# Products with the values moved directly ahead of the next pair's first transposes, and a late pair's transposes issued in two groups

## Chip, cores and metric

The kernel runs on one core of a Trainium2 chip. The metric is device time in microseconds, the median of several executions. One further execution was recorded by the hardware profiler, and its trace is what the rows below come from.

## What is computed

Three layers follow one another. Attention with a block mask (blocks of 64 positions) over 4 batches, 8 heads, 576 positions and 64 dimensions gives 2304 tokens of 512 values. A first MoE layer takes the elementwise maximum of three products and projects it. A second MoE layer routes each token to two of eight experts.

```
scores = q @ k.T / 8, masked to block_i >= block_j;  attn = softmax(scores);  a = attn @ v
x   = maximum(a @ w1, a @ w2, a @ w3) @ w_out
top2 of (x @ w_gate + log1p(exp(x @ w_noise)) * noise);  out = sum over 2 of w * (relu(x @ e1[e]) @ e2[e])
```

## The kernel before, in words

The work on attention is cut into 32 jobs. A job is a batch and a pair of heads, and is either early (the first 256 positions) or late (the positions from 256 on). Jobs 0 to 7 run in a first stage whose order a planner writes out. Jobs 8 to 31 run in the loop at line 1091, and only this loop changes. Their order is the list MIDDLE: `e2 l0 e2 e2 e2 l0 l0 e3 l0 e3 l1 e3 l1 e3 l1 l1 l2 l2 l2 l2 l3 l3 l3 l3`, 8 early and 16 late jobs (the letter, then the batch). The text calls a job of the loop a pair, for its two heads.

A late pair has five query blocks, 4 to 8. For each, `s_block` (line 330) makes the scores with three products (lines 314 to 316), takes the maximum on VectorE (line 320) and the exponential on ScalarE (line 321). `scale` (line 393) divides by the sums on VectorE (lines 395, 396, 400). `t_block` (line 405) transposes the block with TensorE into a PSUM bank (line 403) and copies it to SBUF on ScalarE (line 417, and line 420 on VectorE for a tail). The transposed blocks are the moving operand of `pv` (line 487), the products with the values, which `values` (line 464) issues at line 468: two heads side by side, each on 64 columns of the array. Its result is split in two parts by ScalarE (line 499) and VectorE (line 500) and becomes the input of a MoE unit; late rows of unit 8 are stored through DRAM (line 502). An early pair does the same with `s_early`, `t_early` (transposes at line 427) and `e_values`.

One pass of the loop treats pair j and the scores of pair j + 1. The lists `turn_steps(j)` (line 1042) and `score_steps(j + 1)` (line 1033) are issued alternately, one entry of each, and after each step comes `gap(j)` (line 1048). A gap issues filler: steps of the first MoE layer, generated by `chain` (line 1016), units 2, 4, 1, 6, 3, 5, 7 in this order. A step of `hidden` (line 801) is 24 products of 256 columns (lines 812 to 814) into one PSUM bank, emptied by ScalarE (line 817) or by a maximum on VectorE (line 819); a step of `columns` (line 831) is 18 products of 264 columns (lines 837, 838, 841). Each gap adds 1.0 (pairs 8 to 15) or 1.2 (later pairs) to a budget in the code's own units, and a step takes 2.6 or 2.0 of it. A unit can start only when all pairs of its batch are through, which the set `ready` tells. When no unit is ready, a gap stays empty.

Transposes, products with the values and the products of the filler take PSUM banks from one pool of four, `psT` (line 196). Scores have banks of their own. Loads and stores stand on SP's queue: queries and keys by `scored` (line 1065), values by `load_values` and `load_rest` behind `pv`, and a zero write of the output per pair by `init_out` (line 926). Outside the first stage the builder itself may place an instruction ahead of earlier ones when those are not ready; the code's order is its priority.

Of the kernel before, what the change touches and what calls it, by code (L numbers as in the profile page):

```python
# [38 lines left out]
def _jobs():  # L39
    n, o = {}, []  # L40
    for x in ["e0"] * 4 + ["e1"] * 4 + MIDDLE.split():
        o.append((int(x[0] == "l"), int(x[1]), n.get(x, 0)))
        n[x] = n.get(x, 0) + 1
    return o


JOBS = _jobs()
# [82 lines left out]
def tile_attention_moe_moe(ctx, tc, qT, kT, v, w1, w2, w3, w_out, gates, noise, e1, e2, out):  # L130
# [111 lines left out]
    def bank(kind="m"):  # L242
        n, c = TAGS[kind]
        return (psS if n == "s" else psT).tile([128, 512], F32, name=n, bufs=c)
# [17 lines left out]
    def load_scores(j):  # L262
        q = diagonal(SET[0][0])
        for r in range(2):
            nc.sync.dma_start(q[64 * r:64 * r + 64, :, 64 * r:64 * r + 64],
                              qT[at(j) + r, :, 0:256].rearrange("d (n c) -> d n c", c=64))
        load_keys(j, nc.sync)

    def load_rest(j, eng=None):
        (eng or nc.sync).dma_start(early_set(j)[2], v[at(j):at(j) + 2, :, :2].rearrange("h p c d -> p h (c d)"))  # L270

    def load_job(j):
        i = at(j)
        q = att.tile([128, 320], F32, name="rq")
        k = att.tile([128, S], F32, name="rk")
        nc.sync.dma_start(q, qT[i:i + 2, :, 256:S].rearrange("h d n -> (h d) n"))
        nc.sync.dma_start(k, kT[i:i + 2].rearrange("h d n -> (h d) n"))
        RAW[j] = q, k

    def load_values(j):  # L280
        n = LJ.index(j) % 2
        VV[j] = att.tile([128, 768 if n else 640], F32, name=("rv", "V")[n])[:, :640].rearrange("p (r c) -> p r c", r=2)
        nc.sync.dma_start(VV[j], v[at(j):at(j) + 2].rearrange("h p c d -> p h (c d)"))
# [19 lines left out]
    def prep_job(j):  # L303
        for low in (False, True):
            split_keys(j, low)
        for r in range(2):
            for low in (False, True):
                split_queries(j, r, low)
        RAW.pop(j)
# [20 lines left out]
    def s_block(j, i, c):  # L330
        st = new_stats(j)
        if i == 8:
            ps = psA[0].tile([128, 2, 512], F32, name="a2")
            for r in range(2):
                scores(ps[:, r, 0:288], j, i, 288 * r, 288 * r + 288)
            exps(st, c, ps[:, :, 0:288], PL[8][:, :576].rearrange("p (a b) -> p a b", a=2))
            return
        SB[i] = bank("s")
        ps = SB[i][:, :64 * i + 64]
        scores(ps, j, i, 0, 64 * i + 64)  # L340
        exps(st, c, ps, PL[i][:, :64 * i + 64])
# [32 lines left out]
    def s_early(j, h):  # L374
        e_scores(j, h)
        e_max(j, h)
        e_exp(j, h)

    def e_sums(j):
        st, z = ST[j][:, 1, 0:4], EPS[j, 1][:, 456:460]  # L380
        nc.vector.tensor_scalar(z, st, 1.0e-9, None, op0=OP.add)
        nc.vector.reciprocal(st, z)

    def e_scale(j, on):
        for i, c in EC.items():
            P = early_set(j)[3][:, POFF[i]:POFF[i] + 64 * i + 64]
            x = ST[j][:, 1, c:c + 1]
            if on != "ACT":
                (nc.vector if on == "DVE" else nc.gpsimd).tensor_scalar(P, P, x, None, op0=OP.mult)
            else:  # L390
                nc.scalar.activation(P, P, AF.Copy, scale=x)

    def scale(j, c0, blocks):
        st, z = ST[j][:, 1, c0:c0 + len(blocks)], SB[blocks[0]][:, 500:500 + len(blocks)]
        nc.vector.tensor_scalar(z, st, 1.0e-9, None, op0=OP.add)
        nc.vector.reciprocal(st, z)
        for c, i in enumerate(blocks):
            s = ST[j][:, 1, c0 + c:c0 + c + 1]
            P = PL[i][:, :64 * i + 64]
            nc.vector.tensor_scalar(P, P, s, None, op0=OP.mult)  # L400

    def turn(dst, i, key):
        nc.tensor.transpose(dst, PL[i][:, 128 * key:128 * key + 128], ident)

    def t_block(j, i, tail=None):
        if j not in PT:
            PT[j] = att.tile([128, 2, 4, 320], F32, name=("Ph", "Pl")[LJ.index(j) % 2])
        nk = (i + 2) // 2
        if i == 8:
            nk = 4  # L410
        ps = bank("t")
        for key in range(nk):
            turn(ps[:, 128 * key:128 * key + 128], i, key)
        if tail is not None:
            turn(ps[:, 384:512], tail, 4)
        o = 64 * SLOT[i]
        nc.scalar.activation(PT[j][:, :, :nk, o:o + 64].rearrange("p h k c -> p k h c"),
                             ps[:, :128 * nk].rearrange("p (k h c) -> p k h c", k=nk, h=2), AF.Copy)
        if tail is not None:
            nc.vector.tensor_copy(PT[j][:, :, 3, 192:256], ps[:, 384:512].rearrange("p (h c) -> p h c", h=2))  # L420
# [17 lines left out]
    def t_early(j, key):  # L438
        e_turn(j, key)
        e_copy(j, key, "DVE")  # L440
# [485 lines left out]
    def init_out(j):  # L926
        nc.sync.dma_start(out[256 * j:256 * j + 256].rearrange("(p t) (c d) -> p (t c) d", p=128, d=128),
                          zero[:, None, :].to_broadcast([128, 8, 128]))
# [83 lines left out]
    NJ = len(JOBS)  # L1012
# [11 lines left out]
    def filler(budget):  # L1024
        cost[0] += budget
        while cost[0] > 0:
            c = next(fill, None)
            if c is None:
                cost[0] = 0.0
                return  # L1030
            cost[0] -= c

    def score_steps(j):
        if j >= NJ:
            return []
        if LATE[j]:
            return [lambda: s_block(j, 4, 0), lambda: (s_block(j, 8, 1), scale(j, 0, (4, 8))),
                    lambda: s_block(j, 6, 2), lambda: (s_block(j, 7, 3), scale(j, 2, (6, 7))),
                    lambda: (s_block(j, 5, 4), scale(j, 4, (5,)))]
        return [lambda: s_early(j, 0), lambda: (s_early(j, 1), e_sums(j), e_scale(j, "ACT"))]  # L1040

    def turn_steps(j):
        if LATE[j]:
            return [lambda: (t_block(j, 4, 8), t_block(j, 8)), lambda: None, lambda: (t_block(j, 6), t_block(j, 7)),
                    lambda: None, lambda: t_block(j, 5)]
        return [lambda: (t_early(j, 0), t_early(j, 1))]

    def gap(j):
        filler(PER[j >= 16])
# [3 lines left out]
    def late_after(j):  # L1053
        return next((x for x in LJ if x > j), NJ)
# [4 lines left out]
    def following(j):  # L1059
        if j < 8:  # L1060
            x = next((x for x in range(j + 1, 8) if SETS[x] == SETS[j]), None)
            return x if x is not None else EJ[0] if SETS[j] == 0 else None
        return next((x for x in EJ if x > j), None)

    def scored(j):
        if LATE[j]:
            n = late_after(j)
            if n < NJ:
                prep_job(n)
                n = late_after(n)  # L1070
                if n < NJ:
                    load_job(n)
        elif following(j):
            load_scores(following(j))
# [13 lines left out]
    load_values(late_after(first))  # L1088
    scored(8)
    filler(4.0)  # L1090
    for j in range(8, NJ):
        b, g = JOBS[j][1:]
        T, SS = turn_steps(j), score_steps(j + 1)
        for n in range(max(len(T), len(SS))):
            if n < len(T):
                T[n]()
            if n < len(SS):
                SS[n]()
            gap(j)
        if j + 1 < NJ:  # L1100
            scored(j + 1)
        pv(j)
        if LATE[j]:
            n = late_after(j)
            if n < NJ:
                n = late_after(n)
                if n < NJ:
                    load_values(n)
        elif following(j):
            load_rest(following(j))  # L1110
        gap(j)
        gap(j)
        if j == 10:
            for tt in range(2):
                store(0, tt, C0[tt])
            late.append(route(0, C0["g"]))
        if all(x[:2] != JOBS[j][:2] for x in JOBS[j + 1:]):
            ready.add(2 * b + LATE[j])
        if 8 <= j < 8 + NU:
            init_out(j - 8)  # L1120
    ready.update(range(8))
    while 5 not in done:
        next(fill)
# [355 lines left out]
```

## Time and profile before

| | us |
|---|---|
| median of 3 executions | 974.41 (973.1 to 974.93) |
| the profiled execution, its own time | 970.67 |
| its span, first to last instruction | 968.9 |
| TensorE busy in the span | 957.8 |
| VectorE, ScalarE, GpSimd busy | 434.6, 432.5, 414.2 |

The span is what the views of the trace cover; 1.77 us of the execution lie around it. In a timeline row the first number is the start in us from the span's start, the second the duration. A matmul's duration is modelled and longer than the interval to the next start, since matmuls are pipelined, so what a product costs is read from starts.

### The profile page before, as it was taken

How to read it: one execution, taken by the hardware profiler on the slowest of the kernel's cores; microseconds unless marked ns; L12 is line 12 of the kernel's file. 1: busy time of each engine (PE TensorE's matmuls, PEld its weight loads, DVE VectorE, ACT ScalarE, POOL GpSimd, SP SyncE). 2: the span in 40 equal slices, each digit the busy share in tenths (PEclk: the TensorE clock that was granted, in tenths of full speed). 3: DMA queues.
4: the chain of work that ended last, by engine and by line, in shares of the span. 5: the costliest groups of instructions: out<-in, count | busy, mean ns of one | idle time of the engine just before them, and what ended most of it. 6: DMA issues, size and time to landing. Idle time of an engine off the chain costs nothing. (4 is left out here: it accounts for less than half of the span.)

```text
span 968.9 us, 17049 instructions
## 1 busy us (share of the span) xinstructions
PE 957.8 (99%) x6474; PEld 848.5 (88%) x6474; DVE 434.6 (45%) x1251; ACT 432.5 (45%) x968; POOL 414.2 (43%) x316
## 2 busy tenths in 40 slices
PE   9999999999999999999999999999999999999997
PEld 5866988999989898999999889898898979898895
DVE  7864756656567656643158331314141312222221
ACT  7487545555555545542125145444353434433110
POOL 2596201221322221222251487748565766755302
PEclk9999999999999999999999999999999999999999
DMA  9913822121121311303014459866758594753201
GB/s 325 346 31 94 232 71 73 47 87 53 60 71 47 102 50 41 113 15 123 21 57 154 127 170 235 186 168 179 176 169 182 168 201 143 189 140 124 62 16 56
DMA packets 113734, 118.75 MB, mean 123 GB/s; under 512 B 51164, under 2 KB 85980, under 8 KB 113648
## 3 DMA queue, kind: packets, MB, share of 16 engines
q1 hardware_dynamic: 102304, 88.51, 32.8%
q0 software_dynamic: 10224, 28.32, 10.2%
q8 instruction: 52, 0.85, 0.4%
q10 hardware_dynamic: 1120, 0.79, 0.3%
q14 instruction: 34, 0.28, 0.1%
HBM read 85.35 MB, written 25.24 MB: 114 GB/s over the span
## 5 line engine op out<-in xcount | busy, mean ns | idle before, releaser
L188 POOL TENSOR_TENSOR w<-rw,w 128x1536 fp32r<-128x1536 f32 (+1 forms) x42 | 131.9, 3145 | 65.5 <-ACT w L187 61.3
L828 POOL TENSOR_TENSOR hl<-hm,hh 128x512 fp32r<-128x512 f32 x21 | 27.5, 1309 | 147.4 <-ACT hh L827 146.8
L187 ACT ACTIVATE w<-rw 128x1536 fp32r<-128x1536 f32 (+1 forms) x42 | 55.9, 1344 | 74.4 <-DMA rw<-in_e 53.9
L1173 ACT ACTIVATE xg<-x 128x1024 uint16<-128x1024 uint16 x30 | 40.8, 1373 | 104.4 <-DMA x<-xg 102.9
L1199 PE MATMUL b<-xl,w 128*128 128x256 f32 (+4 forms) x272 | 83.5, 307 | 0.5 <-DVE xl L1189 0.5
L1200 PE MATMUL b<-xh,w 128*128 128x256 f32 (+4 forms) x272 | 83.4, 306 | 0.0
L1198 PE MATMUL b<-xh,w 128*128 128x256 f32 (+4 forms) x272 | 83.3, 306 | 0.0
L812 PE MATMUL t<-xA,w 128*128 128x256 f32 x288 | 83.0, 288 | 0.0
L813 PE MATMUL t<-xA,w 128*128 128x256 f32 x288 | 81.5, 283 | 0.0
L814 PE MATMUL t<-xA,w 128*128 128x256 f32 x288 | 81.3, 282 | 0.0
L1198 PE MATMUL t<-xh,w 128*128 128x256 f32 (+3 forms) x240 | 71.5, 298 | 0.2 <-DVE ht L1203 0.2
L1200 PE MATMUL t<-xh,w 128*128 128x256 f32 (+3 forms) x240 | 71.4, 298 | 0.0
L1199 PE MATMUL t<-xl,w 128*128 128x256 f32 (+3 forms) x240 | 71.3, 297 | 0.0
L1254 POOL DMA_INDIRECT out_rows<-y,isc x37 | 37.4, 1010 | 69.7 <-DVE y L1251 65.1
L812 PE MATMUL t<-xB,w 128*128 128x256 f32 x216 | 61.6, 285 | 0.0
L814 PE MATMUL t<-xB,w 128*128 128x256 f32 x216 | 61.1, 283 | 0.0
L813 PE MATMUL t<-xB,w 128*128 128x256 f32 x216 | 61.0, 282 | 0.0
L819 DVE TENSOR_TENSOR hm<-t,hm 128x512 f32<-128x512 f32 x48 | 33.1, 689 | 60.3 <-PE t L814 53.5
L852 POOL COPY xp<-x 128x1024 uint16<-128x1024 uint16 x18 | 19.4, 1076 | 88.7 <-ACT x L844 48.5
L1246 PE MATMUL b<-w,ht 128*128 128x512 f32 (+3 forms) x144 | 57.0, 396 | 0.0
L1248 PE MATMUL b<-w,ht 128*128 128x512 f32 (+3 forms) x144 | 56.9, 395 | 0.0
L1247 PE MATMUL b<-w,ht 128*128 128x512 f32 (+3 forms) x144 | 56.8, 394 | 0.0
(409 smaller groups left out, 2818.4 us busy)
## 6 DMA issues: line engine op xcount, KB each, us to landing
rw<-in_e SPq DMA_DIRECT2D x32, 768.0 KB
w<-in_w SPq DMA_DIRECT2D x18, 512.0 KB
rw<-in_e SPq DMA_DIRECT2D x16, 512.0 KB
rk<-in_kT SPq DMA_DIRECT2D x16, 288.0 KB
out_rows<-zero SPq DMA_DIRECT2D x9, 512.0 KB
x2d<-x SPq DMA_DIRECT2D x18, 256.0 KB
x2p<-xp SPq DMA_DIRECT2D x18, 256.0 KB
w<-in_w_out SPq DMA_DIRECT2D x6, 512.0 KB
```

What stands on the lines that cost most here:

```text
L187: nc.scalar.activation(t[:, 0, :c], r[:, :c], AF.Copy)
L188: nc.gpsimd.tensor_sub(t[:, 1, :c], r[:, :c], plain(t[:, 0, :c]))
L812: nc.tensor.matmul(ps[:, j], wh, x[:, 0], start=kt == 0, stop=False)
L813: nc.tensor.matmul(ps[:, j], wh, x[:, 1], start=False, stop=False)
L814: nc.tensor.matmul(ps[:, j], wl, x[:, 0], start=False, stop=kt == 3)
L1173: nc.scalar.activation(x.rearrange("p k t -> p (k t)").bitcast(U16).rearrange("p (c h) -> p h c", h=2), tp.rearrange("p (h k) t -> p h (k ...
L1198: nc.tensor.matmul(p, wt1(e, 0, kt, f), th[:, kt, c0:c1], start=kt == 0, stop=False)
L1199: nc.tensor.matmul(p, wt1(e, 0, kt, f), tl[:, kt, c0:c1], start=False, stop=False)
L1200: nc.tensor.matmul(p, wt1(e, 1, kt, f), th[:, kt, c0:c1], start=False, stop=kt == 3)
L1246: nc.tensor.matmul(ps, a, wt2(e, 0, f), start=f == 0, stop=False)
L1247: nc.tensor.matmul(ps, a, wt2(e, 1, f), start=False, stop=False)
L1248: nc.tensor.matmul(ps, l, wt2(e, 0, f), start=False, stop=f == 7)
```

## The change

The products with the values of pair j, with all that followed them in the pass (loads of values, the stores and the routing of unit 0 at j == 10, the mark that a unit is ready), move out of pass j into a function `values_of`. It is called at the start of pass j + 1, ahead of the first transposes, and once behind the loop. The two gaps that stood behind `pv` now stand ahead of it. The third and the fifth entry of a late pair's `turn_steps` become one, so the list has three entries: the blocks 4 and 8, nothing, the blocks 6, 7 and 5. A pass has as many steps as the longer list, so a pass of a late pair ahead of an early one (five) and the last pass have three steps instead of five.

```diff
     def turn_steps(j):
         if LATE[j]:
-            return [lambda: (t_block(j, 4, 8), t_block(j, 8)), lambda: None, lambda: (t_block(j, 6), t_block(j, 7)),
-                    lambda: None, lambda: t_block(j, 5)]
+            return [lambda: (t_block(j, 4, 8), t_block(j, 8)), lambda: None,
+                    lambda: (t_block(j, 6), t_block(j, 7), t_block(j, 5))]
         return [lambda: (t_early(j, 0), t_early(j, 1))]
...
-    for j in range(8, NJ):
+
+    def values_of(j):
         b, g = JOBS[j][1:]
-        T, SS = turn_steps(j), score_steps(j + 1)
-        for n in range(max(len(T), len(SS))):
-            if n < len(T):
-                T[n]()
-            if n < len(SS):
-                SS[n]()
-            gap(j)
-        if j + 1 < NJ:
-            scored(j + 1)
         pv(j)
         if LATE[j]:
             n = late_after(j)
...
         elif following(j):
             load_rest(following(j))
-        gap(j)
-        gap(j)
         if j == 10:
             for tt in range(2):
                 store(0, tt, C0[tt])
             late.append(route(0, C0["g"]))
         if all(x[:2] != JOBS[j][:2] for x in JOBS[j + 1:]):
             ready.add(2 * b + LATE[j])
+
+    for j in range(8, NJ):
+        b, g = JOBS[j][1:]
+        T, SS = turn_steps(j), score_steps(j + 1)
+        if j > 8:
+            values_of(j - 1)
+        for n in range(max(len(T), len(SS))):
+            if n < len(T):
+                T[n]()
+            if n < len(SS):
+                SS[n]()
+            gap(j)
+        if j + 1 < NJ:
+            scored(j + 1)
+        gap(j)
+        gap(j)
         if 8 <= j < 8 + NU:
             init_out(j - 8)
+    values_of(NJ - 1)
     ready.update(range(8))
```

## Rows read from the trace of the kernel before

**Rows 1.** The page, busy us (share of the span) and instructions of each engine.

```profile
PE 957.8 (99%) x6474; PEld 848.5 (88%) x6474; DVE 434.6 (45%) x1251; ACT 432.5 (45%) x968; POOL 414.2 (43%) x316
```

**Rows 2.** Busy time by stretch: length, busy us of each engine, granted clock, DMA.

```profile
97.00:440.00 343.00, 340.82 (x2719) 312.78 (x2718) 213.78 (x676) 180.13 (x481) 76.59 (x64) 1.00 0.26 75
```

**Rows 3.** TensorE's waits, 95 to 440 us: total us, times, longest.

```profile
PE s L314 <- DVE st L396: 1.0, 2, 0.7
PE t L403 <- DVE hm L819: 0.4, 1, 0.4
...
PE t L468 <- ACT Pl L417: 0.2, 1, 0.2
```

**Rows 4.** Timeline, TensorE: an early pair's values between MoE products.

```profile
189.83 0.28 PE L814 MATMUL t<-xA,w 128*128 128x256 f32 x1
190.04 0.87 PE L468 MATMUL t<-pte,kve 128*64 128x256 f32 x8
190.84 0.38 PE L812 MATMUL t<-xA,w 128*128 128x256 f32 x1
191.06 0.28 PE L813 MATMUL t<-xA,w 128*128 128x256 f32 x1
191.18 0.28 PE L814 MATMUL t<-xA,w 128*128 128x256 f32 x1
```

**Rows 5.** TensorE by line, 97 to 440 us: count, busy us, mean ns.

```profile
L468 PE MATMUL t<-Ph,rv 128*64 128x320 f32 (+2 forms) x160 | 18.4, 374 | 0.1
...
L468 PE MATMUL t<-pte,kve 128*64 128x256 f32 (+1 forms) x64 | 7.2, 340 | 0.1
```

**Rows 6.** Timeline, TensorE: eight transposes between MoE products.

```profile
423.05 1.03 PE L403 MATMUL t<-ident,p 128*128 128x128 f32 x8
423.84 0.36 PE L812 MATMUL t<-qe,w 128*128 128x256 f32 x1
424.04 0.28 PE L813 MATMUL t<-qe,w 128*128 128x256 f32 x1
```

**Rows 7.** Timeline, TensorE: values with eight transposes directly behind them.

```profile
147.57 0.87 PE L468 MATMUL t<-pte,kve 128*64 128x256 f32 x8
148.37 1.09 PE L403 MATMUL t<-ident,p 128*128 128x128 f32 x8
149.22 0.36 PE L812 MATMUL t<-xA,w 128*128 128x256 f32 x1
149.42 0.28 PE L813 MATMUL t<-xA,w 128*128 128x256 f32 x1
```

**Rows 8.** Timeline, TensorE: transposes between the halves of an early pair's values.

```profile
268.34 1.09 PE L403 MATMUL t<-ident,p 128*128 128x128 f32 x8
269.37 0.44 PE L468 MATMUL t<-pte,kve 128*64 128x128 f32 x4
```

**Rows 9.** Timeline, TensorE: the scores of block 7 ahead of late values.

```profile
416.70 0.39 PE L315 MATMUL s<-Kh,Ql 128*128 128x512 f32 x1
416.93 0.40 PE L316 MATMUL s<-Kl,Qh 128*128 128x512 f32 x1
417.37 2.28 PE L468 MATMUL t<-Ph,rv 128*64 128x320 f32 x20
```

**Rows 10.** Timeline, TensorE: three transposes (block 5) between MoE products.

```profile
430.56 0.49 PE L403 MATMUL t<-ident,p 128*128 128x128 f32 x3
430.81 0.37 PE L812 MATMUL t<-qe,w 128*128 128x256 f32 x1
431.01 0.28 PE L813 MATMUL t<-qe,w 128*128 128x256 f32 x1
```

**Rows 11.** Timeline, VectorE and TensorE: transposes wait for a bank.

```profile
359.04 0.69 DVE L819 TENSOR_TENSOR hm<-t,hm 128x512 f32<-128x512 f32 x1 [2.02 <-PE t L403]
...
359.78 0.66 PE L403 MATMUL t<-ident,p 128*128 128x128 f32 x4 [0.42 <-DVE hm L819]
```

**Rows 12.** Timeline, SP's queue: zero writes of the output.

```profile
103.95 4.27 SPq L927 DMA_DIRECT2D out_rows<-zero  x3
```

## The prediction

> **What bounds the kernel now.** I read the busy shares first. TensorE is busy for 957.8 of a span of 968.9 us [rows 1], so no other engine sets the end: time is won or lost only where TensorE's own stream gets shorter or gets a hole. Next I read the stretch in which the changed loop runs, about 97 to 440 us. TensorE is busy there for 340.82 of 343.00 us at the full granted clock (1.00, the 2.4 GHz level), VectorE for 213.78, ScalarE for 180.13 [rows 2]. Third come TensorE's waits in that stretch. Three lines hold 1.6 us in four waits: scores behind the statistics of softmax, transposes behind a PSUM bank, and 0.2 us of the products with the values behind a copy [rows 3]. So little is lost in plain waiting. What is left is the price of changing from one kind of product to another, which a busy share hides, because the ends of matmuls are modelled. For that I read start-to-start intervals in the timeline. In a run of MoE products one starts every 0.12 us [rows 4].
>
> **The change, part by part.**
>
> *1. Values directly ahead of transposes.* First the counts: late values products have two lines of 160 records, at 20 to a pair 16 late pairs, and 64 records at 8 to a pair are 8 early ones [rows 5]. That makes 24 groups, of which 23 have a next pair to be put against. The price of one group among MoE products: it starts 0.21 us after the product before it, 0.09 more than the steady 0.12; behind it the first product lasts 0.22 us until the second starts, 0.10 more than steady. From the group's start to the second product's start it is 191.06 - 190.04 = 1.02 us [rows 4]. Eight transposes among products take 424.04 - 423.05 = 0.99 us by the same reading [rows 6]. Where the kernel before happens to have values and eight transposes adjacent, both together take 149.42 - 147.57 = 1.85 us [rows 7]. Apart they are 1.02 + 0.99 less 0.12 for the product that is counted twice, 1.89 us. So adjacency saves 0.04 us. The groups touch transposes already in rows 7, in rows 8 and in one more place, so 20 groups are new: 20 x 0.04 = 0.8 us. The late group of 20 records has no clean twin with eight transposes behind it; I take the same price, since what differs is only what follows the group.
>
> As bounds: at best both ends of every group become free, 23 x (0.09 + 0.10) = 4.4 us. At worst nothing is saved, because the values still differ in kind from their new neighbour. They use the array as 128\*64 where transposes and all other products use 128\*128 (rows 4 and 7 show both forms), so each group still changes the form twice wherever it stands. The Trainium skill, page TensorEngine Tiling (Array Packing), Tiling Modes, Key Properties, says that changing the tiling mode drains TensorE; by that rule alone part 1 would save nothing, and the sum below would be 0.8 us smaller. The trace partly agrees: the price is there on both sides, and beside transposes it is only 0.04 lower. I stay with the measured 0.04.
>
> *2. Two more gaps between a pair's last transposes and its values.* Before, block 5's transposes stand at the end of the pair with only a scores block between them and the values. After, all of a late pair's transposes are out at its third step, and at least three gaps of filler lie between their copies and the values. The only named wait of the values, 0.2 us on ScalarE's copy, goes [rows 3]. Unnamed ones go too: the last 512-column scores product runs 0.44 us until the values start [rows 9]. A 512-column step is 0.23 us (the products before it), with the 0.09 of entry 0.32, so 0.12 was waiting. Between 0.2 us (the named wait alone) and 16 x 0.12 = 1.9 us I take 0.7, nearer the low end, because the view of waits names only one such wait.
>
> *3. Two groups of transposes instead of three.* Three transposes among products take 431.01 - 430.56 = 0.45 us, less one product 0.33, that is 0.11 for each; eight take 0.99 - 0.12 = 0.87, also 0.11 for each [rows 6, 10]. A group has no price of its own, so merging 16 times saves 0. Bounds: 0 and, if its entry cost as much as that of values, 16 x 0.09 = 1.4 us.
>
> *4. Banks.* Products, transposes and values all take PSUM banks of one kind, of which there are four. Blocks 6, 7 and 5 now take three in a row, so the products behind them need the bank of the products just ahead of them, where before one more bank lay between. That bank is freed by VectorE's maximum (or ScalarE's copy). Once in the kernel before that maximum comes late and the second of two transposes groups waits 0.42 us for it [rows 11]. I count one more such wait, +0.4 us. The bounds are 0 (the bank is free in time, as nearly always now) and 16 x 0.42 = 6.7 us. Values plus two transposes banks also make three in a row, but the values alone run 2.28 us [rows 9], which covers the maximum's 0.69 [rows 11].
>
> *5. What else moves.* The evacuation of the values (two ScalarE copies, two VectorE subtractions for a late pair) and the copies of the next transposes now come in one burst. VectorE and ScalarE are 62% and 53% busy [rows 2], and the filler behind covers them; without that cover it is the bank price of part 4. On SP's queue the values' loads, the store of the late rows and, once, four stores of the first unit move two gaps back, past one zero write of the output per pair; those writes are already issued far ahead of their place (three of them at 103.95 us [rows 12]), so nothing new stands in front. The loaded values are needed one pair later by an early pair, two later by a late one, a distance that is the same as before. POOL's two plane copies for the first unit move with their stores, and nobody reads them until the expert stage. Cost 0. The loop has 162 gaps before and 150 after (a late pair ahead of an early one, and the last pair, lose two each). By the code's own prices 5.2 us less filler is emitted in the loop. It runs later in an unbroken stretch, at the same 0.12 us each: 0.
>
> Sum: -0.8 - 0.7 + 0 + 0.4 = **-1.1 us**. The profiled execution took 970.67 us (span 968.9 and 1.77 around it) and would take 969.6. The median of the runs, 974.41, stands 3.7 us above it; carried over, **973.3 us**. A measurement of this kernel can tell about 0.2%, 1.95 us, from no change, so the forecast is "no difference".
>
> **The rivals.**
>
> *Faster, 971.2 us.* The order is loosened enough that all 1.6 us of waits of rows 3 go, and the merged transposes do save half of part 3's bound, with nothing paid back: -0.8 (part 1) - 1.6 - 0.8 = -3.2. For it: the pairs 20 and 21, where by the code's prices the filler has run dry for seven gaps, get filler again, because units are used more slowly. Against it: the first line of rows 3 is scores that wait for softmax statistics; the change leaves those where they are and takes the three transposes away that stood ahead of late scores as cover.
>
> *Slower, 978.4 us.* The bank mechanism of part 4 decides. If the products behind blocks 6, 7 and 5 wait 0.34 us in each of 16 pairs, +5.4 less 1.5 gives about +4. It passes the 0.2% bound from (1.95 + 1.5) / 16 = 0.22 us per pair. For it: rows 11 show that the maximum can queue behind scaling and evacuation, which the change bunches. Against it: once in 16 pairs now.
>
> *The change does not do what it says, 974.4 us.* The emitted order is not what the engines get: in the trace a later pair's eight transposes stand between the two halves of an early pair's values [rows 8], though the text has them apart. If the builder goes on placing whatever is ready, values and transposes may be parted again. Against it: most groups stand where the code puts them, and all inputs of both groups are long ready.
>
> **How the numbers follow.** Forecast 0.40 (all within 0.2%), faster 0.31, slower 0.14, not as written 0.15 (0.12 within, 0.02 faster, 0.01 slower). That gives faster 0.33, same 0.52, slower 0.15. The range runs from the faster rival with some of part 1's upper bound, 970.6, to half of the slower rival with the spread of the shown runs, 976.4. It leaves out most of the slower rival and the far end of the other.
>
> **What would show it.** Right: values start 0.21 us behind a MoE product, the transposes follow without a product between, 20 or more such pairs; the stretch of the loop shorter by about 5 us of filler plus 1 us; the total of waits about as before. Part 3 right: 11 transposes at 0.11 us each. Part 4 wrong: waits of products on hm's maximum, over 0.2 us a pair. The prediction is wrong if adjacency saves over 0.1 us a group, or if a new wait over 2 us in sum shows in that stretch.

## The result, and the profile after

The change made the kernel slower. The median of 20 runs is 977.0 us (972.8 to 985.35), beside 970.61 us (968.73 to 979.84) in 20 runs of the kernel before on the same chip. The ratio is **1.0053, 95% interval 1.0034 to 1.0072**: 0.53%, or 5.1 us. The two medians by themselves lie 6.4 us apart; the text goes by the ratio and its interval. The first three of the 20 runs of the kernel before are those of the table ahead of the prediction (median 974.41), and they lie above 16 of the other 17. Forecast was -0.11%, with a range that ended at +0.2%. The profiled execution took 980.67 us, its span is 978.8 us. That is 10.0 us more than the profiled execution of the kernel before, about twice what the ratio gives, so sums read from these two profiles overstate the loss.

The page's busy times and the windows come first, as in [rows 1, 2].

```profile
PE 960.0 (98%) x6474; PEld 851.9 (87%) x6474; DVE 437.2 (45%) x1251; ACT 429.7 (44%) x968; POOL 413.5 (42%) x316
```

```profile
97.00:440.00 343.00, 338.37 (x2701) 312.46 (x2700) 215.08 (x674) 177.39 (x479) 75.71 (x64) 1.00 0.26 75
```

In the loop's 343 us TensorE is busy 2.45 us less than in [rows 2]. The span grew by 9.9 us and the busy time by 2.2, so most of what is new is holes. The view of TensorE's waits names them. First the loop, 95 to 500 us, as in [rows 3] (total us, times, longest), then the expert stage, 500 to 970 us.

```profile
PE s L315 <- DVE Ql L301: 2.8, 2, 1.5
PE t L403 <- DVE xA L485: 1.1, 1, 1.1
PE s L314 <- DVE st L396: 0.4, 1, 0.4
PE t L812 <- DVE hm L819: 0.3, 1, 0.3
...
PE t L1205 <- DVE ht L1210: 3.5, 2, 2.0
PE b L1205 <- DVE xB L1210: 1.4, 1, 1.4
PE b L1205 <- ACT xh L1195: 0.6, 1, 0.6
...
```

Two things are new in the loop. Scores (L315, the product with the low part of the queries) wait 2.8 us in two waits for the split of the queries on VectorE, line 301, and one group of transposes (L403) waits 1.1 us for VectorE's line 485. The wait of the values for a copy is gone, as forecast. No line of the prediction names the split. The same view of the kernel before has it, in a fourth row that [rows 3] and the prediction's "three lines" leave out:

```profile
PE s L315 <- DVE Ql L301: 0.2, 1, 0.2
```

The expert stage, whose code the change doesn't touch, has more waits too; they come last below.

Here is the first of the two waits, in the timeline: TensorE, then VectorE, then GpSimd. It also shows the adjacency that the change is for.

```profile
145.94 0.34 PE L315 MATMUL s<-Kh,Ql 128*128 128x384 f32 x1
146.12 0.34 PE L316 MATMUL s<-Kl,Qh 128*128 128x384 f32 x1
146.29 0.53 PE L841 MATMUL t<-w,hl 128*128 128x264 f32 x3
146.75 0.87 PE L468 MATMUL t<-pte,kve 128*64 128x256 f32 x8
147.55 1.09 PE L403 MATMUL t<-ident,p 128*128 128x128 f32 x8
148.40 0.39 PE L314 MATMUL s<-Kh,Qh 128*128 128x320 f32 x1
148.63 0.29 PE L314 MATMUL a<-Kh,Qh 128*128 128x288 f32 x1
150.18 0.41 PE L315 MATMUL s<-Kh,Ql 128*128 128x320 f32 x1 [1.26 <-DVE Ql L301]
...
147.44 2.69 DVE L301 SCALAR_TENSOR_TENSOR Ql<-rq,Qh 64x320 fp32r<-64x320 f32 x2 [0.39 <-ACT Qh L299]
...
147.13 1.41 POOL L292 TENSOR_TENSOR Kl<-rk,Kh 128x576 fp32r<-128x576 f32 x1 [4.38 <-ACT Kh L289]
148.48 1.30 POOL L852 COPY xp<-x 128x1024 uint16<-128x1024 uint16 x1
```

How to read it: the split queries of all late pairs share one pair of buffers, so the next late pair's queries can't be split until the last scores of the late pair before (145.94 and 146.12) have read them. Then follow ScalarE's copies and VectorE's two subtractions (`prep_job`, L289 to L301). The next scores need both. In between TensorE has three products, the values and eight transposes as cover, 2.7 us from the L315 at 145.94 to the L314 at 148.63. The two subtractions end at 150.13. An undisturbed one takes 0.49 us (median of the 30, below); these two took 2.69 together. The first lies beside GpSimd's subtraction of the keys, and the second ends 0.35 us behind GpSimd's plane copy (148.48 + 1.30 = 149.78). The other of the two waits, at 271 us, has the same form.

In the kernel before, the same place has the values and eight transposes of [rows 7], and behind them nine MoE products (149.22 to 150.36). Its split was held up as well, but the scores waited almost nothing:

```profile
150.36 0.31 PE L314 MATMUL s<-Kh,Qh 128*128 128x320 f32 x1
...
150.99 0.42 PE L315 MATMUL s<-Kh,Ql 128*128 128x320 f32 x1 [0.18 <-DVE Ql L301]
...
148.91 2.03 DVE L301 SCALAR_TENSOR_TENSOR Ql<-rq,Qh 64x320 fp32r<-64x320 f32 x2 [0.67 <-ACT Qh L299]
```

So the delay was there all along, 2.03 us for two splits, and the filler covered it, though barely: of the 15 late pairs whose queries are split in the loop of the kernel before, three have the split ready only 0.05, 0.05 and 0.25 us before the scores that need it (ends and starts in its trace). The Trainium skill, page SBUF — State Buffer, section Who interferes with whom, says that a VectorE instruction with two SBUF inputs contends with a GpSimd instruction that reads SBUF, and that one of the two blocks fully until the other has ended. The split has two SBUF inputs, and the rows agree, since it is held until GpSimd is through.

### The profile page after: what moved, and what is told of

Same layout as the page of the kernel before. It is cut to its first block, busy times and chain, and to the rows that moved or that the text cites. A ratio compares the mean times of both kernels' runs of the same rounds, so it can differ in the third digit from the quotient of the medians.

```text
span 978.8 us, 17044 instructions
## 1 busy us (share of the span) xinstructions
PE 960.0 (98%) x6474; PEld 851.9 (87%) x6474; DVE 437.2 (45%) x1251; ACT 429.7 (44%) x968; POOL 413.5 (42%) x316
## 5 line engine op out<-in xcount | busy, mean ns | idle before, releaser
L828 POOL TENSOR_TENSOR hl<-hm,hh 128x512 fp32r<-128x512 f32 x21 | 27.1, 1289 | 169.4 <-ACT hh L827 169.4
L1210 DVE SCALAR_TENSOR_TENSOR ht<-t,ht 128x256 fp32r<-128x256 f32 (+3 forms) x56 | 25.9, 462 | 70.9 <-ACT ht L1209 70.9
```

## The experiments

Every ratio below is to the kernel before on the same chip, with its 95% interval; five rounds each unless said.

### The parts of the change alone

**The values moved, the transposes as before.** The change, with the three groups of transposes put back.

```diff
-            return [lambda: (t_block(j, 4, 8), t_block(j, 8)), lambda: None,
-                    lambda: (t_block(j, 6), t_block(j, 7), t_block(j, 5))]
+            return [lambda: (t_block(j, 4, 8), t_block(j, 8)), lambda: None, lambda: (t_block(j, 6), t_block(j, 7)),
+                    lambda: None, lambda: t_block(j, 5)]
```

> Only the move of the values is made; a late pair's transposes stay in three groups. Lost cover (values and transposes now stand where filler stood between the split of the queries and the next scores, so TensorE waits for VectorE): ratio 1.003 to 1.007 to before, and waits of TensorE on the split queries (line 301) of 2 us or more in the loop. Banks or the merged transposes as the cause: 0.998 to 1.001, no such waits. Any new order costs in the expert stage: 1.002 to 1.006, with the loss behind 500 us.

Measured 967.65 us, ratio **0.9968 (0.9952 to 0.9983)**: faster than both kernels, and outside all three ranges that were expected. One wait for the split is there, and no wait in the expert stage.

```profile
PE a L315 <- DVE Ql L301: 1.2, 1, 1.2
```

**The merged transposes in the order of before.** The same edit of `turn_steps` as the change, in the kernel before.

> Only the merge of a late pair's transposes into two groups is made (with the two gaps fewer that follow from it for six pairs); the values stay where they were. Lost cover: 0.998 to 1.002, waits in the loop as before, under 2 us. Three banks in a row as the cause: 1.004 to 1.007, with waits of transposes or products on hm's maximum (line 819) of over 2 us. Any new order costs in the expert stage: 1.002 to 1.006, with the loss behind 500 us.

Measured 974.19 us, ratio 1.0034 (1.0019 to 1.0049); there is no wait on `hm`, by which banks would have shown. Here the price takes another form. With two gaps fewer in six pairs, and the values still at the end of the pass, the values come right behind the copies of the block just transposed:

```profile
PE t L468 <- ACT Pl L417: 1.3, 1, 1.3
PE t L468 <- ACT Ph L417: 1.1, 1, 1.1
```

**The change with the twelve gaps given back.** Two empty steps stand behind the merged group, so that a late pair has five steps again and the loop 162 gaps.

```diff
-                    lambda: (t_block(j, 6), t_block(j, 7), t_block(j, 5))]
+                    lambda: (t_block(j, 6), t_block(j, 7), t_block(j, 5)), lambda: None, lambda: None]
```

> The change with two empty steps added to a late pair's list, so that the loop has 162 gaps as before. Fewer gaps as the cause: back to 0.998 to 1.001. Lost cover: 1.002 to 1.006, since the gaps stand ahead of the values either way and the waits on line 301 stay. Any new order costs in the expert stage: 1.002 to 1.006 with the loss behind 500 us.

Measured 973.2 us, ratio 1.0023 (1.0004 to 1.0042). So the change's +5.1 us splits, at about 971 us, into -3.1 (values), +5.3 (merge: 1.0023 against 0.9968) and +2.9 (the missing gaps: 1.0053 against 1.0023). By the intervals each of the last two is uncertain by about 2.5 us. The scores wait for the split four times, and behind ScalarE's half of it once:

```profile
PE s L315 <- DVE Ql L301: 2.2, 4, 1.0
...
PE s L314 <- ACT Qh L299: 0.5, 1, 0.5
```

**Less filler ahead of the loop.** In the kernel before, `filler(4.0)` ahead of the loop became `filler(1.4)`, which shifts the phase of the filler's steps.

> The kernel before with 1.4 in place of 4.0 units of filler ahead of the loop, one MoE step less there; nothing else. Any new order costs in the expert stage: 1.002 to 1.006 here too, with the loss behind 500 us. Lost cover or banks: 0.998 to 1.002, neither is touched.

Measured 972.05 us, ratio 1.0008 (0.9992 to 1.0025): no difference. This one shift of phase does not bring the loss; others were not tried.

### GpSimd's part: one operation moved

**The plane copies on ScalarE**, in the change and in the kernel with the values alone moved. They are the operation that held up the second split above.

```diff
-        nc.gpsimd.tensor_copy(planes, x2.bitcast(U16).rearrange("p (d h) -> p h d", h=2))
+        if u == NU - 1:
+            nc.gpsimd.tensor_copy(planes, x2.bitcast(U16).rearrange("p (d h) -> p h d", h=2))
+        else:
+            nc.scalar.activation(planes, x2.bitcast(U16).rearrange("p (d h) -> p h d", h=2), AF.Copy)
```

> The change, with the plane copy of units 0 to 7 (line 852) on ScalarE in place of GpSimd. VectorE held up by GpSimd (split queries of 1.4 us twice in a row where Kl and the plane copy follow each other): no split query over 1.5 us and none that follows a second one of over 1 us because of line 852; waits of TensorE on line 301 fall from 2.8 us to under 1.5; ratio to before 1.001 to 1.004. Only the order counts: waits of the same size on line 301 or elsewhere in the loop, 1.004 to 1.007.

> Only the move of the values, and the plane copy of units 0 to 7 on ScalarE. VectorE held up by GpSimd: as fast as the move alone or 1 us faster, 0.995 to 0.998. Only the order counts, or ScalarE's 25 us more are felt: 0.998 to 1.002.

The change went from 1.0053 to 1.0027 (1.001 to 1.0043), at 972.33 us; the wait for the split fell from 2.8 to 1.3 us. The values alone gained nothing, 0.9984 (0.9967 to 1.0002). By the waits the copy is part of the price, not all of it; the ratios point the same way, but the intervals of the change with and without the edit overlap.

**Both kernels once more**, unchanged, one profile each, to see which waits repeat.

> The changed kernel once more, for a second profile. The loss behind 509 us comes from the built order: again 6 us or more between the first transposes of expert 0 and the last expert, with waits on line 1210 at the same products. It varies with each execution's transfers: 2 to 5 us, at other products; the loop's waits on line 301 (2.8 us) are as before in both cases.

> The kernel before once more, for a second profile. Loss from the built order: waits in the expert stage under 1 us again. It varies with each execution's transfers: up to 3 us of them. Waits in the loop 1.8 us as before in both cases.

The change again took 2.8 us in two waits on L301, 1.1 on L485. The kernel before again had no such wait over 0.2 us, but now 3.1 us in one wait of L1198 on `ht` in the expert stage. The loop's waits repeat; the expert stage's come and go in both kernels.

### Merge or gaps

**Block 5 one step earlier, but in a step of its own.** The values moved, 162 gaps; the edit is shown against the kernel with the values alone moved. From the change with its gaps given back it differs in one thing: block 5 comes one step later, so that the scores of block 6 and a gap part it from the blocks 6 and 7.

```diff
-                    lambda: None, lambda: t_block(j, 5)]
+                    lambda: t_block(j, 5), lambda: None]
```

> The values moved as in the change; three groups of transposes as before, but block 5's comes one step earlier, straight in the step behind that of the blocks 6 and 7 (162 gaps). It stands between the run that moves the values alone (ratio 0.9968) and the change with two empty steps appended (1.0023), and differs from the second only in that one gap of filler parts block 5 from 6 and 7. If the merge costs because eleven transposes and three banks come in one step: ratio near 0.997, 0.995 to 0.999. If it costs because block 5's transposes no longer stand as cover ahead of the next pair's last scores, whatever they are grouped with: near 1.002, 1.000 to 1.004, with the scores' wait for VectorE's split of the queries (L301) at 2 us or more in the loop.

Measured 967.13 us, ratio **0.9972 (0.9956 to 0.9988)**. So it costs nothing that block 5 leaves its place ahead of a pair's last scores. What costs is what parts this kernel from the change with its gaps given back: block 5 put together with 6 and 7. Whether that is the merge itself, or that block 5 then comes two steps early, was not told apart: an unmerged block 5 two steps early with 162 gaps was not run. The scores' wait on L301 is gone. The timeline of both kernels at one pair shows why. First the change with its gaps given back, then this one, from the last scores of one late pair to the first of the next (in this one the products between 269.81 and 273.40 are left out).

```profile
270.34 0.34 PE L316 MATMUL s<-Kl,Qh 128*128 128x384 f32 x1
270.64 1.03 PE L403 MATMUL t<-ident,p 128*128 128x128 f32 x8
272.18 0.42 PE L314 MATMUL s<-Kh,Qh 128*128 128x320 f32 x1 [0.50 <-ACT Qh L299]
...
273.68 0.42 PE L315 MATMUL s<-Kh,Ql 128*128 128x320 f32 x1 [0.96 <-DVE Ql L301]
```

```profile
269.52 0.34 PE L316 MATMUL s<-Kl,Qh 128*128 128x384 f32 x1
269.81 1.03 PE L403 MATMUL t<-ident,p 128*128 128x128 f32 x8
...
273.40 0.31 PE L314 MATMUL s<-Kh,Qh 128*128 128x320 f32 x1
...
273.80 0.31 PE L315 MATMUL s<-Kh,Ql 128*128 128x320 f32 x1
```

From the last scores to the next it is 1.84 us with the merge, 0.50 of it a wait, and 3.88 without. Here 23 filler products stand behind the eight transposes (270.60 to 273.40); with the merge the filler comes only at 276.9 us, behind the first scores of the next pair. Filler comes in steps of 24 or 18 products, and the two kernels differ in the side of those first scores on which one step falls. By what rule the builder places it there is not shown.

**Three groups in three consecutive steps.** Again shown against the kernel with the values alone moved: nothing merged, but a late pair has three steps and the loop 150 gaps, as in the change.

```diff
-            return [lambda: (t_block(j, 4, 8), t_block(j, 8)), lambda: None, lambda: (t_block(j, 6), t_block(j, 7)),
-                    lambda: None, lambda: t_block(j, 5)]
+            return [lambda: (t_block(j, 4, 8), t_block(j, 8)), lambda: (t_block(j, 6), t_block(j, 7)),
+                    lambda: t_block(j, 5)]
```

> The values moved; three groups of transposes, unmerged, but in three consecutive steps, so that a late pair has three steps and the loop 150 gaps, as in the change. If the twelve gaps that go cost by themselves (the change without them is 0.3% faster than with them): 1.000, between 0.998 and 1.002, and the first transposes of expert 0 come 0.8 to 2 us later against the last filler than with 162 gaps. If the gaps cost nothing and the merge all: 0.997, 0.995 to 0.9985, loop waits under 2 us.

Measured 973.72 us, ratio 1.0034 (1.0011 to 1.0056), outside what was expected on either side. The gaps cost by themselves, and 0.66% here, so the split above into merge and gaps depends on the order in which they are taken: with the gaps first it is 6.4 us for them and 1.8 for the merge. The loop's waits on these two lines are nearly those of the change:

```profile
PE s L315 <- DVE Ql L301: 2.8, 2, 1.5
PE t L403 <- DVE xA L485: 0.8, 1, 0.8
```

**Amount or place of the filler.** In the kernel just shown each gap's budget times 1.08; in the kernel with the values alone moved, times 150/162.

> The values moved, three groups of transposes in three consecutive steps (150 gaps, ratio 1.0034), each gap's budget 1.08 times larger, so that the loop emits as much filler as with 162 gaps. If it is the amount of filler in the loop that costs: near the 162-gap kernels, 0.995 to 0.9985. If it is the place of the gaps (a late pair ahead of an early one has two gaps fewer between its values and the next scores, or the transposes stand closer): 1.001 to 1.005, with the scores' wait on L301 still over 2 us in the loop.

> The values moved, transposes as before (162 gaps, ratio 0.9968), each gap's budget cut to 150/162, so that the loop emits as little filler as with 150 gaps. If the amount costs: 1.000 to 1.004. If the place of the gaps costs: 0.995 to 0.9985.

Measured 1.0001 (0.9985 to 1.0017), between the two ranges expected, and 0.998 (0.9959 to 1.0). Giving the amount back recovers about half; taking it away costs 0.12%, which the intervals don't tell from nothing. Neither reading is enough alone.

### GpSimd's work out of the loop

Four orders, each with the keys' subtraction (L292) and the low part (L828) given to VectorE and the plane copies (L852, units 0 to 7) to ScalarE as above, and the kernel before with the same edit as control.

```diff
-            nc.gpsimd.tensor_sub(QK[j][1], k, plain(QK[j][0]))
+            nc.vector.tensor_sub(QK[j][1], k, plain(QK[j][0]))
...
-            (nc.vector if u == NU - 1 else nc.gpsimd).tensor_sub(l, m, plain(a))
+            nc.vector.tensor_sub(l, m, plain(a))
```

> The values moved, transposes as before, and the loop's GpSimd work on SBUF (the keys' subtraction L292, the low part L828, the plane copies of the units 0 to 7) given to VectorE, VectorE and ScalarE. Nothing is left out. VectorE then has some 36 more operations of about 0.5 us each but none held up by GpSimd. If VectorE held by GpSimd is what makes scores wait: L301 takes about 0.5 us everywhere, no wait on it in the loop; ratio 0.995 to 0.998 beside 0.9968 with GpSimd. If VectorE becomes too full: waits on maxima and splits, ratio over 0.999.

> The same three pieces of GpSimd's work moved away in the change with two empty steps appended (162 gaps, merged transposes, ratio 1.0023). If the merge costs because it brings scores up to where VectorE is still held by GpSimd: within 0.2% of the run of the values alone without GpSimd's work, so 0.995 to 0.999, and the waits on L301 (2.2 us) are gone. If the merge costs through banks, order or the cover of scores whatever GpSimd does: 0.4% to 0.6% above that run, 1.000 to 1.003.

> The three consecutive steps with 150 gaps (1.0034) with the loop's GpSimd work on SBUF given to VectorE and ScalarE. With 162 gaps and without that work the ratio was 1.0000. If the missing gaps cost because scores come up while GpSimd holds VectorE: within 0.2% of that, 0.998 to 1.002, no wait on L301. If they cost in another way (order around the last units, the expert stage): 1.003 to 1.008.

> The whole change (1.0053) with the loop's GpSimd work on SBUF given to VectorE and ScalarE. If GpSimd holding VectorE is what both the merge and the missing gaps cost by: 0.998 to 1.002. If only the merge costs by it and the gaps by something else: 1.002 to 1.005. If neither: over 1.005.

> The kernel before with the loop's GpSimd work on SBUF given to VectorE and ScalarE, the control for the four variants with the same edit (0.9986 to 1.0007). If GpSimd's work costs only where scores are late by the change, the edit brings the kernel before nothing or a small loss: 1.000 to 1.004, and the change then counts as 0 to 0.4% faster on that ground. If the edit itself is worth the 0.5 to 0.7% that it brought the change, independent of the order: 0.993 to 0.996.

| order | GpSimd as it is | its work moved |
|---|---|---|
| before | 1 | 1.0008 (0.9988 to 1.0028) |
| values moved | 0.9968 | 1.0000 (0.9978 to 1.0021) |
| values, merge, 162 gaps | 1.0023 | 1.0007 (0.9987 to 1.0027) |
| values, no merge, 150 gaps | 1.0034 | 1.0002 (0.9984 to 1.002) |
| the change | 1.0053 | 0.9986 (0.997 to 1.0001) |

On the left the four changed orders lie 0.85% apart, on the right 0.21%, less than their intervals. The edit by itself brings the kernel before nothing. So the merge and the gaps cost only together with GpSimd's work. One wait on L301 is left among these five, 0.6 us in the order without the merge. That the values alone lose their 0.3% with this edit was not expected (0.995 to 0.998 was); with the merge and 162 gaps, too, the ratio lies above the 0.995 to 0.999 expected for this cause, though within 0.2% of the values alone, as was expected. VectorE has more to do then, and the loop has one new wait, 0.9 us of early scores (L356) behind L485; why the gain goes stays open.

**The keys' subtraction alone** given to VectorE, in the change; the other two stay on GpSimd.

> The change with the keys' subtraction alone (L292) given to VectorE; the low part L828 and the plane copies L852 stay on GpSimd. If the split of the queries is late because it runs beside that one subtraction: the wait on L301 (2.8 us in two, up to 1.5) goes and the ratio is 0.9985 to 1.002, as with all three moved. If the other two hold VectorE as much (L400 of 3.2 us behind L828): 1.002 to 1.005, with the wait of L403 on xA (1.1) still there.

Measured 969.98 us, ratio **0.9987 (0.9966 to 1.0007)**: one line takes back the whole loss. The kernel before with this one line moved was not run; with all three pieces moved it is 1.0008. It is the cleanest of the runs, because TensorE's order at the pair shown above stays the same (the three products L841 left out):

```profile
144.38 0.34 PE L315 MATMUL s<-Kh,Ql 128*128 128x384 f32 x1
...
145.19 0.87 PE L468 MATMUL t<-pte,kve 128*64 128x256 f32 x8
145.99 1.09 PE L403 MATMUL t<-ident,p 128*128 128x128 f32 x8
...
147.07 0.29 PE L314 MATMUL a<-Kh,Qh 128*128 128x288 f32 x1
147.20 0.41 PE L315 MATMUL s<-Kh,Ql 128*128 128x320 f32 x1
...
145.47 0.76 DVE L292 TENSOR_TENSOR Kl<-rk,Kh 128x576 fp32r<-128x576 f32 x1
146.15 1.00 DVE L301 SCALAR_TENSOR_TENSOR Ql<-rq,Qh 64x320 fp32r<-64x320 f32 x2
```

The cover is the same 2.7 us (144.38 to 147.07), but keys and queries together are through in 1.68 us (145.47 to 147.15), and nothing waits. All 30 splits of the stretch now take the same time, first the change, then this kernel (ns: least, median, most):

```profile
L301 DVE SCALAR_TENSOR_TENSOR Ql<-rq,Qh x30: 472/490/1592, 111.1 to 404.3; 64x320 fp32r<-64x320 f32 x30
```

```profile
L301 DVE SCALAR_TENSOR_TENSOR Ql<-rq,Qh x30: 475/484/492, 110.1 to 397.9; 64x320 fp32r<-64x320 f32 x30
```

### What stays open: the expert stage

The traces tell how much of the loss lies in the loop. Here the loop is counted from its first scores to the first transposes of expert 0, and the rest from there to the end of TensorE's last product (us, from starts in the traces; the two kernels each have two profiles).

| kernel | loop | behind it |
|---|---|---|
| before | 410.5 and 409.6 | 453.5 and 458.9 |
| the change | 412.6 and 411.8 | 462.1 and 457.9 |
| the change, keys' subtraction on VectorE | 407.4 | 455.3 |
| before, GpSimd's work moved | 410.7 | 456.0 |
| the change, GpSimd's work moved | 407.7 | 456.1 |

The loop's part of the loss is 1.3 to 3.0 us. The rest of the 5.1 lies outside it, and behind the loop two profiles of one kernel differ by 4 to 5 us. With GpSimd's work moved in both, the change's loop is 3.0 us shorter than the other's, which is the direction that was forecast; each is one profile, and the intervals of the ratios (0.9986 and 1.0008) overlap.

In the change 6.4 us of waits stand behind 500 us, 0.7 in the kernel before. One of them, 2.0 us, is ScalarE's queue: a copy of expert weights stands ahead of the `relu` that TensorE needs, and waits for the weights.

```profile
649.33 1.38 ACT L1180 ACTIVATE xg<-x 128x1024 uint16<-128x1024 uint16 x1 [8.22 <-DMA x<-xg]
650.57 2.41 ACT L187 ACTIVATE w<-rw 128x1024 fp32r<-128x1024 f32 x2
...
659.09 1.49 ACT L187 ACTIVATE w<-rw 128x1536 fp32r<-128x1536 f32 x1 [5.47 <-DMA rw<-in_e]
660.48 0.46 ACT L1209 ACTIVATE ht<-t 128x368 fp32r<-128x368 f32 x1
```

ScalarE had stood 8.22 us for gathered rows before that, and the weights' own read (line 174) could start only when the subtraction on GpSimd that follows these copies (line 188) had freed a buffer, at 654.12. A wait of this kind, 3.1 us, stands in the second profile of the kernel before too, so it is not the change's alone. It is longer than 0.6 us in neither of the two kernels at 0.997. With GpSimd's work as it is, the waits behind 500 us add up to 1.1 to 6.4 us in five profiles with 150 gaps and to 0 to 3.3 in seven with 162, so the ranges overlap. Whether the missing gaps make them likelier, and how, was not tried.

## Why the prediction was wrong

**Part 1 was right.** Values stand directly ahead of transposes 21 times (20 or more were forecast), they start 0.21 us behind a product, and the values moved alone make the kernel 0.32% faster. That is 3.1 us where the sum had 1.5 for parts 1 and 2. Whether the sizes were right is not shown: in its profile the loop (from the first scores at 96.84 to the first transposes of expert 0 at 506.38) takes 409.5 us, 1.0 less than in the first profile of the kernel before (98.31 to 508.81) and no less than in the second.

**Part 2 was right as to its wait:** no wait of L468 is left.

**Part 3 is the step that failed, and part 5 with it.** Part 3 costed the merge at 0, with bounds of 0 and 1.4 us of gain, from the price of a transposes group on TensorE (0.11 us each). That price is right. The merge costs 5.3 us nonetheless, as measured with 162 gaps. No loss was put into the bounds, because the step asked only what the instructions cost and not what a new order does to the work that covers a wait. What the runs show in its place: less work of TensorE between one late pair's last scores and the next scores (at the pair above 1.84 us, where it is 3.88 with block 5 in a step of its own), less than the split of the queries needs beside GpSimd (3.3 us there, from the last scores to its end). The prediction had come near: its faster rival says that the change "takes the three transposes away that stood ahead of late scores as cover". It gave that no price, and it is not quite the cover that counted: with block 5 taken from the last scores, but in a step of its own, the kernel stays at 0.9972.

**Part 4 had the right kind of wait and the wrong cause.** One transposes group waits 1.10 us for a bank, where 0.4 was taken. VectorE, which frees the bank by L485, was held in a scaling (L400) through two of GpSimd's instructions. The timeline of the change, TensorE, VectorE, GpSimd:

```profile
246.68 0.98 PE L403 MATMUL t<-ident,p 128*128 128x128 f32 x7 [1.10 <-DVE xA L485]
...
243.13 3.16 DVE L400 TENSOR_SCALAR p<-p,st 128x384 f32<-128x384 f32 x1
246.21 0.41 DVE L485 TENSOR_TENSOR xA<-t,xA 128x256 fp32r<-128x256 f32 x1
...
243.39 1.31 POOL L828 TENSOR_TENSOR hl<-hm,hh 128x512 fp32r<-128x512 f32 x1
244.62 1.44 POOL L292 TENSOR_TENSOR Kl<-rk,Kh 128x576 fp32r<-128x576 f32 x1
```

The slower rival, banks behind the blocks 6, 7 and 5 in every pair, did not happen: no product waits on `hm` for more than 0.3 us in the whole loop. The sign came out on its side by another mechanism.

**Part 5.** "Twelve gaps fewer: 0, the filler runs later at the same price" holds for the filler, not for what the gaps were covering. Unmerged, with 150 gaps instead of 162, the kernel goes from 0.9968 to 1.0034. The part looked at VectorE's 62% and called it covered. That share says nothing of one operation that takes 1.45 us instead of 0.49 in front of scores.

The prediction's own test, that it is wrong "if a new wait over 2 us in sum shows in that stretch", was met: 2.8 us on L301. The view of waits of the kernel before showed 0.2 us of it in one row, which the prediction passed over; where a wait is just covered, there is no row. What showed its size were the splits' durations: 26.8 us for 30 in the loop of the kernel before, 894 ns in the mean (groups by line), where an undisturbed one takes 490.

## What to carry to other kernels

Before work is moved or gaps are closed, look for the near misses: for each producer that the critical engine needs, take the distance between its end and its consumer's start, and its own spread of durations. Here a median of 490 ns with a mean of 894 was the sign of a neighbour on GpSimd, and a single wait of 0.2 us on the same producer was the sign that the cover was used up. A delay that is covered today is paid as soon as the cover moves; the cheaper remedy is to take the delay away (one subtraction moved to VectorE: 1.0053 to 0.9987), or to move only the part that takes little of the cover (the values: 0.9968).

## What was not expected of the hardware

A VectorE operation that starts first can still be the one held up: L400 above starts at 243.13, GpSimd's L828 at 243.39, and L400 ends 0.23 us behind the second GpSimd instruction, 3.16 us after its start; the kernel before has the same at 302.35 us (L400 of 3.20 us, GpSimd from 302.63 on). With GpSimd's work moved, no L400 of the loop takes over 0.72 us in the change and 0.55 in the kernel before. The Trainium skill, same page and section, says of VectorE in a mode with two ports, which it lists as open to a `tensor_scalar` like L400, that whoever issues first keeps the ports for the whole instruction and the other blocks. By the recorded starts it was the other way round here, and the hold lasted through two instructions back to back. The records don't show when an engine asks for its ports, so the two need not contradict each other.

The same subtraction of the keys takes 1.42 us on GpSimd and 0.76 on VectorE, so even the work itself was better placed there.

A long wait in the expert stage also touches the clock: behind the 2.0 us wait at 659 us the granted clock of 660 to 665 us (windows) is 0.71 in the mean, so part of that stretch ran at the lower level of 1.2 GHz, where it is 1.00, the 2.4 GHz level, for the kernel with the values alone moved. In the second profile of the kernel before it is 0.51 for 655 to 660 us, behind the wait of 3.1 us. So such a wait costs more than its own length: in that stretch products of 368 columns start every 0.31 us, and every 0.17 us in the kernel with the values alone moved.
